# First layer-norm block of a transformer layer: V weights loaded as full-row slices, and two tiles transposed before they are centred

## The chip, the cores and the metric

The kernel runs on one core of one Trainium2 chip. The metric is the device time of one execution in microseconds. Before the change, three runs gave 692.64, 690.5 and 692.12 us, a median of 692.12 us. Data are bf16, accumulation is f32.

## The reference

A whole transformer layer is computed on 2048 rows of width 1024, with 32 heads of 32 columns, a causal window of 256 keys, and an MLP of width 3584:

```python
h  = x + attention(layernorm(x) @ wqkv) @ wo     # softmax over keys q-255 .. q
h2 = h + silu(layernorm(h) @ w1) @ w2
```

The layer norm has no weights: `(x - mean) / sqrt(var + 1e-5)`.

## The kernel before

The rows are worked in four blocks of 512, each of four tiles of 128 rows. TensorE (PE) needs the normalized rows transposed, `lnT_b`: eight pieces (kt) of 128 columns, each with the block's 512 rows beside one another. From these come V, tile by tile and half by half of 512 columns (`v_group`, L249: eight matmuls of 128x512), and Q and K, 128 output columns for all four tiles at a time (`qk_group`, L259). Attention of a block runs between the dense matmuls of the next one, then come the output projection (L280) and the MLP (L673, L710).

Every engine takes its instructions in the order in which the program writes them (`tc.manual_schedule()`), so the order of the lines is the order of each engine's queue: PE (matmuls and transposes), DVE (VectorE), ACT (ScalarE), POOL (GpSimd), and SP, which issues nearly all DMAs. Accumulators in PSUM are taken in turn by `next_acc` (L239): two banks normally, four while the first block's V is made (L476), and six from the MLP on (L668), when the four banks of the attention scores (`sc`) join. The counter that chooses the bank, `acc_n`, runs through the whole program.

The change lies in the first block, which has nothing to hide its start behind:

- **Loads (L155 to L163).** SP issues tile 0 of x, then V's first 512 columns in four pieces of 256 KB (two kt each), tile 2, the other 512 columns in two pieces of 512 KB with tile 3 between them, and the first quarter of the Q and K weights. ACT issues tile 1.
- **Warming (L172 to L176).** Two calls of `busy` run f32 matmuls on zeros, of 512 and 384 columns, before the data are there.
- **Tiles 0 and 1.** The mean is summed half on ACT and half on DVE (L464), DVE centres the tile in four quarters (L471), PE transposes it in pairs of kt (`turn_first`, L220), and ACT or DVE copies the transposes out of PSUM into `lnT_b`. These tiles aren't scaled yet: PE multiplies centred rows by V's weights (L497 for the first 512 columns, L513 for the others), and the eviction to `v` on ACT multiplies with 1/std (L532, L538). The variance is a squaring pass on ACT (`var_first`, L477), and later DVE normalizes both tiles in place (`norm_first`, L484) and a transposing DMA (`ln_transpose`, L211) overwrites their part of `lnT_b` for Q and K.
- **Tile 2** is normalized in full first: statistics on DVE (`ln_stats`, L182), root on ACT (L215), reciprocal and normalization on DVE (L218, L208), PE transposes (`turn_some`, L515), copies on ACT and DVE.
- **Tile 3** goes the same way but is transposed by DMA.
- **Order.** `ORDER` (L42) lists PE's steps: a pair `(j, h)` transposes two kt of tile j, a triple `(j, k0, k1)` multiplies kt k0 to k1 of tile j by V's first half. Then follow, in the order of the lines L506 to L546, the second half for tiles 0 and 1 in two parts (`half_pair`) around tile 2's transposes and first half, tile 2's second half, and tile 3. At the end SP loads the other Q and K weights (L541), ACT loads the table of Exp (L544), and `qk_group` begins (L582).

Of the kernel before, what the change touches and what calls it, by code (L numbers as in the profile page):

```python
# [8 lines left out]
BF16 = mybir.dt.bfloat16  # L9
F32 = mybir.dt.float32  # L10
I32 = mybir.dt.int32
ACT = mybir.ActivationFunctionType
ALU = mybir.AluOpType

P = 128
# [23 lines left out]
    [(1, "Y", 2), (2, "C", 1), (3, "Y", 3)],  # L39
]  # L40
SPLIT = [(0, 8), (8, 16), (16, 21), (21, 27), (27, 32)]
ORDER = [  # L42
    (0, 0), (0, 1), (0, 2), (0, 0, 2), (0, 3), (0, 2, 4), (1, 0), (0, 4, 6), (1, 1), (1, 2), (1, 3), (1, 0, 4),
    (1, 4, 6), (0, 6, 8), (1, 6, 8),
]


# [1 line left out]
def kernel(  # L49
# [88 lines left out]
    def load_x(b, j, queue=nc.sync):  # L138
        queue.dma_start(out=x_ring[(b % 2) * 4 + j], in_=x2d[(b * 4 + j) * P:(b * 4 + j + 1) * P, :])

    def load_wqkv(c0, parts=1, queues=(nc.sync,)):
        dst = wqk[:, :, c0:c0 + 512] if c0 < 2 * D else wv[:, :, c0 - 2 * D:c0 - 2 * D + 512]
        n = KT // parts
        for k in range(0, KT, n):
            queues[k // n % len(queues)].dma_start(out=dst[:, k:k + n, :], in_=wqkv_v[:, k:k + n, c0:c0 + 512])
# [8 lines left out]

    load_x(0, 0)  # L155
    load_x(0, 1, nc.scalar)
    load_wqkv(2 * D, 4)
    load_x(0, 2)
    for k in (0, 4):
        nc.sync.dma_start(out=wv[:, k:k + 4, 512:1024], in_=wqkv_v[:, k:k + 4, 2 * D + 512:3 * D])  # L160
# [11 lines left out]
    def busy(n):  # L172
        nc.tensor.matmul(o_ps[0][:].rearrange("p (a c) b -> p a (c b)", c=2)[:, 0:n], lhsT=warm, rhs=wide[:, 0:n], start=True, stop=True)

    for n in (4, 3):
        busy(n)  # L176


# [35 lines left out]
    def ln_root(st, rs, j):  # L214
        nc.scalar.activation(out=rs[:, j:j + 1], in_=st[:, j, 1:2], func=ACT.Sqrt, bias=eps[:], scale=1.0)  # L215

    def ln_recip(rs, j):
        nc.vector.reciprocal(out=rs[:, j:j + 1], in_=rs[:, j:j + 1])  # L218

    def turn_first(j, h, src, copy):  # L220

        for i in range(2):
            kt = h * 2 + i
            nc.tensor.transpose(out=tp_ps[h][:, i * P:(i + 1) * P], in_=src[:, kt * P:(kt + 1) * P], identity=ident[:])
        n = 2 if j or h else 1
        for i in range(0, 2, n):
            copy(out=lnT_b[0][:, h * 2 + i:h * 2 + i + n, j * P:(j + 1) * P],
                 in_=tp_ps[h][:, i * P:(i + n) * P].rearrange("p (k q) -> p k q", q=P))

    def ln_tiles(tag):  # L230
        st = small.tile([P, 4, 2], F32, name=f"st_{tag}", tag=f"st_{tag}")
# [7 lines left out]
    def next_acc():  # L239
        acc_n[0] += 1  # L240
        return acc_banks[acc_n[0] % len(acc_banks)]
# [213 lines left out]


    st, rs = ln_tiles("a")
    x_mid = [view(r_e, 1024 + 1024 * j, 1024) for j in range(2)]
    scrap = view(r_e, 3072, 1024)
    scrap_v = view(r_e, 4096, 512)  # L460
    mean = small.tile([P, 6], F32, name="mean")
    var = small.tile([P, 2], F32, name="var")

    def half_mean(j, h, engine):  # L464
        x, m = x_ring[j][:, h * 512:(h + 1) * 512], mean[:, j * 2 + h:j * 2 + h + 1]
        if engine is nc.scalar:
            engine.activation(out=scrap[:, 0:512], in_=x, func=ACT.Identity, scale=-1.0 / D, accum_out=m)
        else:
            engine.tensor_scalar(out=scrap_v, in0=x, scalar1=-1.0 / D, scalar2=None, op0=ALU.mult, op1=ALU.add, accum_out=m)

    def center(j):  # L471
        for h in range(4):
            out, in0 = (x[j][:, h * 256:(h + 1) * 256] for x in (x_mid, x_ring))
            nc.vector.tensor_scalar(out=out, in0=in0, scalar1=mean[:, j * 2:j * 2 + 1], scalar2=mean[:, j * 2 + 1:j * 2 + 2], op0=ALU.add, op1=ALU.add)

    acc_banks += [o[:].rearrange("p a b -> p (a b)") for o in o_ps]  # L476
    def var_first(j):  # L477

        nc.scalar.activation(out=scrap, in_=x_ring[j], func=ACT.Square, bias=mean[:, j + 4:j + 5], scale=1.0, accum_out=var[:, j:j + 1])

    def root_first(j):
        nc.scalar.activation(out=rs[:, j:j + 1], in_=var[:, j:j + 1], func=ACT.Sqrt, bias=eps[:], scale=1.0 / D)

    def norm_first(j):  # L484
        nc.vector.tensor_scalar(out=x_ring[j], in0=x_ring[j], scalar1=mean[:, j + 4:j + 5], scalar2=rs[:, j:j + 1], op0=ALU.add, op1=ALU.mult)

    for j in range(2):
        half_mean(j, 1, nc.scalar)
        half_mean(j, 0, nc.vector)
        center(j)  # L490
    nc.vector.tensor_tensor(out=mean[:, 4:6], in0=mean[:, 0:4:2], in1=mean[:, 1:4:2], op=ALU.add)
    first = [next_acc() for _ in range(2)]
    for step in ORDER:
        if len(step) == 3:
            j, k0, k1 = step
            for kt in range(k0, k1):
                nc.tensor.matmul(first[j], lhsT=lnT_b[0][:, kt, j * P:(j + 1) * P], rhs=wv[:, kt, 0:512], start=(kt == 0), stop=(kt == KT - 1))  # L497
        else:
            turn_first(*step, x_mid[step[0]], dve if step[0] and step[1] > 1 else act)
    var_first(0)  # L500
    ln_stats(x_ring[2], st, 2)
    ln_root(st, rs, 2)
    var_first(1)
    ln_recip(rs, 2)
    ln_norm(x_ring[2], st, rs, 2)
    pair = [next_acc() for _ in range(2)]  # L506

    def half_pair(k):
        for j in range(2):
            for kt in range(k, k + 4):  # L510
                if (k, j, kt) == (0, 1, 3):
                    turn_some(0, 2, 0, 2)
                nc.tensor.matmul(pair[j], lhsT=lnT_b[0][:, kt, j * P:(j + 1) * P], rhs=wv[:, kt, 512:1024], start=(kt == 0), stop=(kt == KT - 1))  # L513

    def turn_some(bank, j, k0, k1, copy=act):  # L515
        for kt in range(k0, k1):
            nc.tensor.transpose(out=tp_ps[bank][:, (kt - k0) * P:(kt - k0 + 1) * P], in_=x_ring[j][:, kt * P:(kt + 1) * P], identity=ident[:])
        copy(out=lnT_b[0][:, k0:k1, j * P:(j + 1) * P], in_=tp_ps[bank][:, 0:(k1 - k0) * P].rearrange("p (k q) -> p k q", q=P))

    ln_stats(x_ring[3], st, 3)  # L520
    half_pair(0)
    turn_some(1, 2, 2, 4)
    turn_some(2, 2, 4, 8, dve)
    ln_root(st, rs, 3)
    for j in range(2):
        root_first(j)
    ln_recip(rs, 3)
    ln_norm(x_ring[3], st, rs, 3)
    ln_recip(rs, 0)
    ln_recip(rs, 1)  # L530
    for j in range(2):
        nc.scalar.activation(out=v[:, j, 0:16, 0:DH], in_=first[j].rearrange("p (h d) -> p h d", d=DH), func=ACT.Identity, scale=rs[:, j:j + 1])  # L532
    v_group(0, 2, 0, act, acc=tp_ps[3][:].bitcast(F32))
    norm_first(0)
    norm_first(1)
    half_pair(4)
    for j in range(2):
        nc.scalar.activation(out=v[:, j, 16:32, 0:DH], in_=pair[j].rearrange("p (h d) -> p h d", d=DH), func=ACT.Identity, scale=rs[:, j:j + 1])  # L538
    for j in (3, 0, 1):
# [4 lines left out]
    nc.scalar.activation(out=dummy[:], in_=eps[:], func=ACT.Exp)  # L544
    v_group(0, 3, 0, act)
    v_group(0, 3, 1, act)  # L546
# [216 lines left out]
```

## Time and profile before

| | |
|---|---|
| runs | 692.64, 690.5, 692.12 us; median 692.12 us |
| profiled execution, first to last instruction (span) | 688.4 us |
| median less span | 3.7 us |
| PE busy | 674.8 us, 98% |
| DVE, ACT, POOL busy | 292.2, 244.0, 160.6 us |
| granted TensorE clock, mean | 1.000 |
| DMA | 61.48 MB, mean 89 GB/s |

The profile is that of one execution; for the profiled execution itself only the span is given. A busy PE isn't PE at its peak, since matmuls overlap in the pipeline. In a timeline row stand the start, the time to the end of the last instruction of the group, the engine, the line, the operation, the output and inputs, the count, and in brackets the idle time of the engine before and what ended it. A row of the chain gives start, length, what, and how many.

### The profile page before, as it was taken

Reading aid. Unit: us, or ns where it says so; the run is one execution under the profiler, and the core shown is the slowest. Engines: PE = TensorE matmul, PEld = TensorE weight load, DVE = VectorE, ACT = ScalarE, POOL = GpSimd, SP = SyncE. Lnnn points to the kernel's source line nnn. Section 1 sums busy time; section 2 is a strip of 40 time slices with the busy share of each in tenths; the row PEclk is TensorE's granted clock in tenths of the full one; section 3 lists DMA queues with packets and bytes.
Section 4 is the critical chain, followed back from the end, with each engine's and each line's share of the span. In section 5 each row is a group of like instructions: output and inputs, shape, how many; then the busy total and the mean of one; then the engine's idle time right before and its main releaser. Section 6 shows DMA issues by size and latency. Waiting matters only on the chain.

```text
span 688.4 us, 14116 instructions
## 1 busy us (share of the span) xinstructions
PE 674.8 (98%) x5890; PEld 341.9 (50%) x6004; DVE 292.2 (42%) x614; ACT 244.0 (35%) x465; POOL 160.6 (23%) x295
## 2 busy tenths in 40 slices
PE   9999999999999999999999999999999999999998
PEld 4445555555555555544444444444444444444445
DVE  5267647744444459434316133342233251333111
ACT  6326666667666666421300033300133100233000
POOL 1016665566666656400000000000000000000000
PEclk9999999999999999999999999999999999999999
DMA  8842242136241888781023310023300124100110
GB/s 272 262 64 69 42 89 51 29 60 186 71 131 28 254 246 236 177 313 61 17 88 113 83 39 0 1 91 72 82 0 1 34 83 91 39 1 1 30 39 24
DMA packets 78640, 61.48 MB, mean 89 GB/s; under 512 B 52464, under 2 KB 62704, under 8 KB 78576
## 3 DMA queue, kind: packets, MB, share of 16 engines
q1 hardware_dynamic: 78432, 60.31, 31.7%
q8 instruction: 47, 0.77, 0.5%
q10 hardware_dynamic: 144, 0.26, 0.1%
q14 instruction: 17, 0.14, 0.1%
HBM read 39.85 MB, written 8.39 MB: 70 GB/s over the span
## 4 chain that ended last, share of the span: by engine, by line
PE 98%; issue 1%; DMA 0%; DVE 0%; DVEq 0%
PE hacc L673 19%; PE acc L259 16%; PE hacc L710 14%; PE acc L710 14%; PE acc L673 9%; PE acc L280 7%; PE acc L249 6%; PE o_ps L392 5%; PE sc L312 3%; PE hacc L280 1%; PE sc L364 1%; PE sc L338 1%; PE o_ps L249 1%; DMA r_o<-in_A_x_dram 0%; PE acc L497 0%
## 5 line engine op out<-in xcount | busy, mean ns | idle before, releaser
L382 POOL TENSOR_SCALAR_AFFINE_SELECT r_e<-r_e 128x512 bf16<-128x512 bf16 (+1 forms) x288 | 157.6, 562 | 123.6 <-ACT r_e L372 60.3
L710 PEld LDWEIGHTS <-r_a 128*128 128x128 bf16 x952 | 90.9, 98 | 103.0
L673 PEld LDWEIGHTS <-r_w 128*128 128x128 bf16 x896 | 87.3, 98 | 104.8
L673 PE MATMUL hacc<-r_e,r_w 128*128 128x512 bf16 x468 | 104.9, 379 | 0.5
L710 PE MATMUL hacc<-r_a 128*128 128x512 bf16 (+1 forms) x496 | 100.2, 361 | 0.4
L710 PE MATMUL acc<-r_a 128*128 128x512 bf16 (+1 forms) x439 | 94.5, 372 | 0.5
L324 ACT ACTIVATE r_e<-sc 128x768 bf16<-128x768 f32 x96 | 78.2, 814 | 47.6 <-PE sc L312 46.6
L682 ACT ACTIVATE r_n<-hacc 128x512 f32<-128x512 f32 x30 | 17.9, 597 | 178.9 <-PE hacc L673 177.8
L259 PEld LDWEIGHTS <-r_w 128*128 128x128 bf16 x512 | 47.1, 98 | 55.0 <-issue 1.0
L261 DVE CAST r_a<-acc 128x512 bf16<-128x512 f32 x56 | 38.7, 692 | 57.4 <-PE acc L259 54.8
L259 PE MATMUL acc<-r_t,r_w 128*128 128x512 bf16 x233 | 56.5, 380 | 2.4 <-issue 1.7
L259 PE MATMUL acc<-r_w 128*128 128x512 bf16 x240 | 56.0, 379 | 1.5 <-issue 0.9
L392 PEld LDWEIGHTS <-r_e 128*128 128x128 bf16 x1440 | 47.4, 96 | 17.9
L392 PE MATMUL o_ps<-r_a,r_e 128*128 128x33 bf16 x1440 | 48.1, 178 | 0.0
L280 PE MATMUL acc<-r_o,r_a 128*128 128x512 bf16 x188 | 46.3, 380 | 1.9 <-issue 1.1
L673 PE MATMUL acc<-r_e,r_w 128*128 128x512 bf16 x191 | 43.3, 379 | 0.2
L725 DVE SCALAR_TENSOR_TENSOR r_t<-acc,r_t 128x512 bf16<-128x512 f32 (+1 forms) x16 | 10.6, 665 | 69.3 <-PE acc L710 63.9
L325 ACT ACTIVATE r_e<-sc 128x256 bf16<-128x256 f32 x96 | 37.6, 392 | 0.0
L280 PEld LDWEIGHTS <-r_a 128*128 128x128 bf16 x256 | 23.4, 98 | 27.0
L683 DVE SCALAR_TENSOR_TENSOR r_a<-r_n,hacc 128x512 bf16<-128x512 f32 x30 | 20.6, 687 | 33.1 <-ACT r_n L682 33.1
L683 DVE SCALAR_TENSOR_TENSOR r_a<-r_a,hacc 128x512 bf16<-128x512 f32 x30 | 20.6, 687 | 31.2 <-ACT r_a L682 31.2
L725 DVE SCALAR_TENSOR_TENSOR r_t<-hacc,r_t 128x512 bf16<-128x512 f32 (+1 forms) x18 | 11.6, 647 | 51.7 <-PE hacc L710 51.7
(104 smaller groups left out, 546.7 us busy)
## 6 DMA issues: line engine op xcount, KB each, us to landing
r_w<-in_B_w_dram SPq DMA_DIRECT2D x8, 896.0 KB, 5.9
r_a<-in_B_w_dram SPq DMA_DIRECT2D x7, 1024.0 KB, 8.0
r_w<-in_A_wqkv_dram SPq DMA_DIRECT2D x4, 1024.0 KB, 9.0
h_dram<-r_t SPq DMA_DIRECT2D x16, 256.0 KB, 2.4
r_t<-h_dram SPq DMA_DIRECT2D x16, 256.0 KB, 2.9
out_dram<-r_t SPq DMA_DIRECT2D x31, 128.0 KB, 1.7
r_o<-in_A_x_dram SPq DMA_DIRECT2D x15, 256.0 KB, 4.2
r_e<-h_dram SPq DMA_DIRECT2D x3, 1024.0 KB, 5.6
```

The source lines that it names most:

```text
L249: nc.tensor.matmul(acc, lhsT=lnT_b[b % 2][:, kt, j * P:(j + 1) * P], rhs=wv[:, kt, c * 512:(c + 1) * 512], start=(kt == 0), stop=(kt == KT ...
L259: nc.tensor.matmul(acc, lhsT=wqk[:, kt, col0:col0 + P], rhs=lnT_b[b % 2][:, kt, :], start=(kt == 0), stop=(kt == KT - 1))
L261: copy(out=(qT, kT)[which][b][:, g, :], in_=acc)
L280: nc.tensor.matmul(acc, lhsT=qT[b][:, g, j * P:(j + 1) * P], rhs=wo[:, g, c * 512:(c + 1) * 512], start=(g == 0), stop=(g == G - 1))
L324: nc.scalar.activation(out=tri[:, :, :, 64:256], in_=both, func=ACT.Exp, scale=scale)
L325: nc.scalar.activation(out=e[:, 1024:1280].rearrange("p (h q) -> p h q", q=P), in_=bank[:, :, 192:320], func=ACT.Exp, scale=scale)
L382: nc.gpsimd.affine_select(out=dst, in_=src, pattern=[[0, n] for n in dst.shape[1:-1]] + [[sgn, P]], compare_op=ALU.is_ge if upper else ALU ...
L392: nc.tensor.matmul(o_ps[pair][:, qt * 2 + hh, 0:VW], lhsT=chunk_of(i, bank, piece, pair, hh), rhs=v[:, b * 4 + kt, g * 4 + pair * 2 + hh, ...
L673: nc.tensor.matmul(acc, lhsT=w1[:, kt, ft * P:(ft + 1) * P], rhs=ln2T[b][:, kt, :], start=(kt == 0), stop=(kt == KT - 1))
L683: nc.vector.scalar_tensor_tensor(out=gT[:, ft, :], in0=th, scalar=1.0, in1=acc, op0=ALU.add, op1=ALU.mult)
L710: nc.tensor.matmul(acc[:, 0:c1 - c0], lhsT=gT[:, ft, j * P:(j + 1) * P], rhs=w2[ft // 4][:, ft % 4, c0:c1], start=(ft == 0), stop=(ft == F ...
L725: nc.vector.scalar_tensor_tensor(out=t_out[j % 2][:, c0:c1], in0=acc[:, 0:c1 - c0], scalar=0.5, in1=t_in[j % 2][:, c0:c1], op0=ALU.mult, o ...
```

## The change

- V's weights come in eight slices of 256 KB, one kt with all 1024 columns each (rows of 2 KB in place of 1 KB). Tile 2 is issued behind slice 3 and tile 3 behind slice 4.
- The second warming call is cut from 384 columns to 128.
- Of tiles 0 and 1, PE transposes kt 2 to 7 as loaded, before the mean is known. Kt 0 and 1 are centred first (`center_first`) and transposed then (`turn_mid`). For the others, the negative mean is brought from a column to a row by two small matmuls against the identity (`spread_mean`; the mean split into two bf16 parts), copied to SBUF (`m_row`), and added by DVE while it copies the transposes out of PSUM (`center`), two kt at a time.
- Tile 0's mean is still made by halves on ACT and DVE; tile 1's is one pass on ACT.
- Tile 2's mean, variance and root are on ACT, behind tile 0's variance; tile 1's variance comes after them. Tile 3's statistics stay on DVE.
- PE's order (`FIRST`): each slice of weights is used for both column halves of tiles 0 and 1 when its turn comes, in four accumulators; `(1,)` and `(2,)` stand for tile 1's centred transposes and its mean row with everything that follows on DVE and ACT; the steps with "turn" transpose half of tile 2 each. Then tile 2's and tile 3's V as whole groups.
- Tile 3's transposing DMA is issued ahead of those of tiles 0 and 1 as before, all of them written behind tile 2's steps. `next_acc` is called six times in the block in place of seven.

```diff
-ORDER = [
...
+FIRST = [
+    (0, 0), (0, 1), (1,), (0, 2), (2,), (0, 3), (1, 0), (1, 1), (1, 2), (1, 3),
+    (0, 4), (1, 4), (0, 5), (1, 5), (0, 6), (1, 6), (2, 0, 4, "turn"), (0, 7), (2, 4, 8, "turn"), (1, 7),
 ]
...
     load_x(0, 0)
     load_x(0, 1, nc.scalar)
-    load_wqkv(2 * D, 4)
-    load_x(0, 2)
-    for k in (0, 4):
-        nc.sync.dma_start(out=wv[:, k:k + 4, 512:1024], in_=wqkv_v[:, k:k + 4, 2 * D + 512:3 * D])
-        if k == 0:
-            load_x(0, 3)
+    for k in range(KT):
+        nc.sync.dma_start(out=wv[:, k, :], in_=wqkv_v[:, k, 2 * D:3 * D])
+        if k in (3, 4):
+            load_x(0, k - 1)
     load_wqkv(0)
...
-    for n in (4, 3):
+    for n in (4, 1):
         busy(n)
...
+    x_mid = [view(r_e, 1024 + 256 * j, 256) for j in range(2)]
+    m_row = [view(r_e, 4608 + 256 * j, 256).bitcast(F32) for j in range(2)]
+    spread = [t[:].bitcast(F32) for t in tp_ps[2:]]
+
+    def neg_mean(out, x):
+        nc.scalar.activation(out=scrap[:, 0:x.shape[-1]], in_=x, func=ACT.Identity, scale=-1.0 / D, accum_out=out)
+
+    def low_part(j):
+        m = mean[:, j:j + 1]
+        nc.vector.tensor_tensor(out=low[:, j:j + 1], in0=m, in1=m.bitcast(BF16)[:, 1:2], op=ALU.subtract)
+
+    def spread_mean(j):
+        parts = (mean[:, j:j + 1].bitcast(BF16)[:, 1:2], low[:, j:j + 1])
+        for n, m in enumerate(parts):
+            nc.tensor.matmul(spread[j][:, 0:P], lhsT=m.to_broadcast([P, P]), rhs=ident[:], start=(n == 0), stop=(n == 1))
+
+    def turn(bank, off, j, k0, k1):
+        for kt in range(k0, k1):
+            nc.tensor.transpose(out=tp_ps[bank][:, off + (kt - k0) * P:off + (kt - k0 + 1) * P],
+                                in_=x_ring[j][:, kt * P:(kt + 1) * P], identity=ident[:])
+
+    def center_first(j, a, b=None):
+        nc.vector.tensor_scalar(out=x_mid[j], in0=x_ring[j][:, 0:256], scalar1=a, scalar2=b, op0=ALU.add, op1=ALU.add if b is not None else ALU.bypass)
...
+    def center(j, k0):
+        m = m_row[j]
+        nc.vector.tensor_tensor(out=lnT_b[0][:, k0:k0 + 2, j * P:(j + 1) * P],
+                                in0=tp_ps[j][:, k0 * P:(k0 + 2) * P].rearrange("p (k q) -> p k q", q=P),
+                                in1=bass.AP(tensor=m.tensor, offset=m.offset, ap=[m.ap[0], [0, 2], m.ap[1]]), op=ALU.add)
...
+    turn(0, 2 * P, 0, 2, 8)
+    turn(1, 2 * P, 1, 2, 8)
+    neg_mean(mean[:, 6:7], x_ring[0][:, 512:1024])
+    nc.vector.tensor_scalar(out=scrap_v, in0=x_ring[0][:, 0:512], scalar1=-1.0 / D, scalar2=None, op0=ALU.mult, op1=ALU.add,
+                            accum_out=mean[:, 7:8])
+    neg_mean(mean[:, 1:2], x_ring[1])
+    center_first(0, mean[:, 6:7], mean[:, 7:8])
+    nc.vector.tensor_tensor(out=mean[:, 0:1], in0=mean[:, 6:7], in1=mean[:, 7:8], op=ALU.add)
+    low_part(0)
+    turn_mid(0)
+    copy_mid(0, dve)
+    spread_mean(0)
+    dve(out=m_row[0], in_=spread[0][:, 0:P])
+    center(0, 2)
+    center_first(1, mean[:, 1:2])
+    low_part(1)
+    center(0, 4)
+    first = [[next_acc() for _ in range(2)] for _ in range(2)]
+
+    def slices(j, k, *cs):
+        for c in cs or (0, 1):
+            nc.tensor.matmul(first[j][c], lhsT=lnT_b[0][:, k, j * P:(j + 1) * P], rhs=wv[:, k, c * 512:(c + 1) * 512],
+                             start=(k == 0), stop=(k == KT - 1))
+
+    for n, step in enumerate(FIRST):
+        if step == (1,):
+            turn_mid(1)
+            copy_mid(1, act)
+            center(0, 6)
+        elif step == (2,):
+            spread_mean(1)
+            act(out=m_row[1], in_=spread[1][:, 0:P])
+            for k in (2, 4, 6):
+                center(1, k)
+            var_first(0)
+            neg_mean(mean[:, 2:3], x_ring[2])
+            var_first(2)
+            root_first(2)
+            ln_stats(x_ring[3], st, 3)
+            ln_root(st, rs, 3)
+            ln_recip(rs, 2)
+            norm_first(2)
+            ln_recip(rs, 3)
+            ln_norm(x_ring[3], st, rs, 3)
+            var_first(1)
+        elif len(step) == 4:
+            j, k0, k1, _ = step
+            turn(k0 // 4, 0, j, k0, k1)
+            dve(out=lnT_b[0][:, k0:k1, j * P:(j + 1) * P], in_=tp_ps[k0 // 4][:, 0:512].rearrange("p (k q) -> p k q", q=P))
         else:
+            slices(*step)
     for j in range(2):
         root_first(j)
+        ln_recip(rs, j)
+    ln_transpose(x_ring[3], lnT_b[0], 3)
     for j in range(2):
+        norm_first(j)
     for j in range(2):
+        for c in range(2):
+            nc.scalar.activation(out=v[:, j, c * 16:(c + 1) * 16, 0:DH], in_=first[j][c].rearrange("p (h d) -> p h d", d=DH),
+                                 func=ACT.Identity, scale=rs[:, j:j + 1])
+    for j in range(2):
         ln_transpose(x_ring[j], lnT_b[0], j)
     for c0 in (D, 512, D + 512):
         load_wqkv(c0)
-    v_group(0, 2, 1, act)
+    v_group(0, 2, 0, act, acc=spread[0])
+    v_group(0, 2, 1, act, acc=spread[1])
     nc.scalar.activation(out=dummy[:], in_=eps[:], func=ACT.Exp)
```

More of the change, by code (lines that the diff above doesn't have):

```diff
@@ L218, in ln_recip @@
         nc.vector.reciprocal(out=rs[:, j:j + 1], in_=rs[:, j:j + 1])
[L220 to L228, printed above, removed]
     def ln_tiles(tag):
@@ L457 @@
     st, rs = ln_tiles("a")
-    x_mid = [view(r_e, 1024 + 1024 * j, 1024) for j in range(2)]
     scrap = view(r_e, 3072, 1024)
     scrap_v = view(r_e, 4096, 512)
[L461 to L474, printed above, removed]
-    acc_banks += [o[:].rearrange("p a b -> p (a b)") for o in o_ps]
+    mean = small.tile([P, 8], F32, name="mean")
+    low = small.tile([P, 2], BF16, name="low")
+    var = small.tile([P, 3], F32, name="var")
+    acc_banks += [o[:].rearrange("p a b -> p (a b)") for o in o_ps]
@@ L500 @@
[L500 to L524, printed above, removed]
+        nc.vector.tensor_scalar(out=x_ring[j], in0=x_ring[j], scalar1=mean[:, j:j + 1], scalar2=rs[:, j:j + 1], op0=ALU.add, op1=ALU.mult)
```

33 lines of the change are left out of this document (6 added, 27 removed).

## The prediction

> **What bounds the kernel now.** I read the page first: the share of each engine and the chain that ended last.
>
> ```profile
> span 688.4 us, 14116 instructions
> PE 674.8 (98%) x5890; PEld 341.9 (50%) x6004; DVE 292.2 (42%) x614; ACT 244.0 (35%) x465; POOL 160.6 (23%) x295
> PE 98%; issue 1%; DMA 0%; DVE 0%; DVEq 0%
> ```
>
> PE carries 98% of the chain. An edit therefore counts only if it alters how much PE does, or when PE has to stand still. The change touches the first 21 us, so the second view is the chain of that stretch (start, length, what, count).
>
> ```profile
> 0.81 2.79 DMA r_o<-in_A_x_dram
> ...
> 4.43 0.36 DVE r_e L474
> ...
> 4.83 0.80 PE tp L224 x6
> 5.63 0.56 PE acc L497 x2
> ...
> 12.04 0.14 issue
> ...
> 17.31 3.45 PE o_ps L249 x16
> 20.76 0.43 PE acc L259 x2
> ```
>
> The reader sees a load, a mean, a centring, and then PE without a break but 0.14 us from 4.83 to 20.76, where the Q and K products (L259) begin. The wait at 12.04 is the only gap left to close. So the change is worth what it does to one moment: when the first L259 matmul can start. Whatever stands after that moves with it. A 512-column matmul costs 3.45/16 = 0.216 us.
>
> The third view is the timeline of the engines, with durations of single instructions.
>
> ```profile
> 4.83 0.55 PE L224 MATMUL tp<-ident,r_e 128*128 128x128 bf16 x4 [0.35 <-DVE r_e L474]
> 7.21 0.50 PE L224 MATMUL tp<-ident,r_e 128*128 128x128 bf16 x6
> L224 PE MATMUL tp<-ident,r_e x16: 219/219/311, 4.8 to 7.5; 128*128 128x128 bf16 x16
> 5.58 0.61 PE L497 MATMUL acc<-r_w 128*128 128x512 bf16 x2
> 20.60 15.70 PE L259 MATMUL acc<-r_w 128*128 128x512 bf16 x70
> ```
>
> One transpose lasts 0.219 us, but they follow one another closely: (0.50 - 0.22)/5 = 0.056 us apart at 7.21, and (0.55 - 0.22)/3 = 0.11 us apart at 4.83. PE runs at half pace until about 5.2 us. The stretch that I sum runs from the first V matmul (5.58) to the first L259 (20.60): 15.02 us. In it lie 64 V matmuls, 64 x 0.216 = 13.82, and the 20 transposes left of 24, 20 x 0.056 = 1.12; the sum is 14.94, so 0.08 us are slack.
>
> **The change part by part.**
>
> *PE work.* After the first V matmul the changed kernel still has the 64 matmuls, but of transposes only tile 1's two centred ones and tile 2's eight (10 x 0.056 = 0.56), and the second mean's two spreading matmuls of 128 columns (0.11; not in this trace, priced as transposes, the nearest row; at 512 columns they would cost 0.43). Sum 13.82 + 0.56 + 0.11 + 0.08 = 14.57 against 15.02: **-0.45 us**. The twelve raw transposes and the first spread come before.
>
> *The start.* Tile 0's mean is made as before, and the first centring still ends near 4.8. But PE's queue holds tile 1's six raw transposes ahead of the two centred ones, and these wait for tile 1's load.
>
> ```profile
> 3.62 0.69 DVE L469 TENSOR_SCALAR_CACHE_REDUCE r_e<-r_o 128x512 bf16<-128x512 bf16 x1 [2.54 <-DMA r_o<-in_A_x_dram]
> 4.00:5.00 1.00, 0.65 (x3) 0.13 (x2) 0.89 (x5) 0.96 (x4) 0.00 (x0) 1.00 1.03 315
> 5.00:6.00 1.00, 1.00 (x8) 0.49 (x7) 1.00 (x4) 0.84 (x6) 0.00 (x0) 1.00 1.06 366
> 10.00:11.00 1.00, 1.00 (x6) 0.41 (x5) 0.90 (x3) 1.00 (x3) 0.00 (x0) 1.00 1.10 350
> ```
>
> Tile 0 is there at 3.60. The windows (last column GB/s) show 315 to 366, so a piece of 256 KB takes 0.72 to 0.83 us: tile 1 comes at about 4.35, its transposes at half pace take 6 x 0.11 = 0.66, and the centred pair starts near 5.0 instead of 4.83: **+0.17 us**, first matmul at 5.75.
>
> *Weights.* The order is now x0, x1, slices 0 to 3, x2, slice 4, x3, slices 5 to 7. By 0.72 to 0.78 a piece the slices come at about 5.1, 5.8, 6.6, 7.3, 8.8, 10.3, 11.0, 11.8. PE asks for slice 0 at 5.75, 1 at 6.18, 2 at 6.72 (after two transposes), 3 at 7.27, 4 at 9.4, 5 at 10.3, 6 at 11.1, 7 after tile 2's first transposes. Slices 2, 3 and 5 are close. From 0 to 0.4 us; I take **+0.1**. SP's three extra issues cost 1.95/4 = 0.49 us each on a queue that is otherwise waiting:
>
> ```profile
> 1.27 1.95 SPq L145 DMA_DIRECT2D r_w<-in_A_wqkv_dram  x4
> SPq L160 <- DMA r_w<-in_A_wqkv_dram: 0.3, 1, 0.3
> 13.39 4.18 SPq L212 DMA_TRANSPOSE r_w<-r_o  x3
> ```
>
> The second row is an issue that had to wait for an earlier landing, and the changed kernel has more such issues. Still, six pieces are under way by then, so the engines aren't short of work.
>
> *Centring at the copy.* Tile 0's copy moves to DVE and each later pair of slices is one DVE addition of a 128x256 piece in PSUM and the mean row.
>
> ```profile
> 7.70 0.49 DVE L227 COPY r_w<-tp 128x256 bf16<-128x256 bf16 x2 [0.27 <-PE tp L224]
> 281.11 0.42 DVE L404 TENSOR_TENSOR r_n<-o_ps,recip 128x256 bf16<-128x256 f32 x1
> ```
>
> Such an addition isn't in this trace; a copy of that size takes 0.25, a multiplication out of PSUM 0.42, and I take the middle, 0.34, since it has the copy's bf16 source and the multiplication's second operand. DVE does copy, mean row, addition, tile 1's centring, its low part, addition, addition: from 5.4 to about 7.2, ahead of PE by 0.3 us or more at every use. Tile 1's additions start at 7.8 and end at 8.9, used from 8.5, two slices at a time. I cost them at nothing; the cover is PE's own work on slices 0 to 3.
>
> *Tile 2's statistics.* Before, they were on DVE and beside ACT's variances. Now all are in ACT's queue: mean row of tile 1, variance of tile 0, mean of tile 2, variance of tile 2, root. Each is a pass over 1024 columns.
>
> ```profile
> 7.79 1.15 ACT L479 ACTIVATE r_e<-r_o,mean 128x1024 bf16<-128x1024 bf16 x1
> 8.84 0.19 ACT L479 ACTIVATION_READ_ACCUMULATOR r_e<-r_o,mean 128x1 f32 x1
> 9.74 0.29 ACT L215 ACTIVATE rs_a<-st_a,eps 128x1 f32<-128x1 f32 x1 [0.71 <-DVE st_a L188]
> 10.07 0.16 DVE L218 RECIPROCAL rs_a<-rs_a 128x1 f32<-128x1 f32 x1 [0.36 <-ACT rs_a L215]
> 10.27 0.55 DVE L208 TENSOR_SCALAR r_o<-r_o,st_a,rs_a 128x1024 bf16<-128x1024 bf16 x1
> 11.00 0.31 PEld L517 LDWEIGHTS <-r_o 128*128 128x128 bf16 x2
> 6.98 0.37 ACT L227 COPY r_w<-tp 128x256 bf16<-128x256 bf16 x1 [0.27 <-PE tp L224]
> 10.73 1.28 DVE L180 BATCH_NORM_STATS2 ln_st<-r_o 128x6 f32<-128x512 bf16 x2
> 12.04 0.21 DVE L188 BATCH_NORM_AGGREGATE st_a<-ln_st 128x2 f32<-128x12 f32 x1
> ```
>
> A pass with its read is 8.84 + 0.19 - 7.79 = 1.24 us. From root to PE's weight load is 11.00 - 9.74 = 1.26. PE ends the second spread at 5.75 + 0.86 + 0.11 + 0.1 + 0.43 + 0.11 = 7.36. ACT sees it 0.2 later and copies 128x128 in about 0.26 (less than the 0.37 of 128x256): 7.82. Three passes: 11.54. Tile 2 is on PE's doorstep at 12.80. PE reaches its transposes after 28 matmuls: 5.75 + 6.05 + 0.11 + 0.11 + 0.1 = 12.12. **It waits 0.7 us**, with four matmuls of slice 7 queued behind that don't need tile 2. Bounds: 0 if the passes overlap more or PE is late anyway, 1.2 if DVE, which takes tile 3's statistics (1.28 + 0.21 after x3's landing) ahead of the reciprocal, is late too.
>
> *Behind it.*
>
> ```profile
> r_w<-r_o SPq DMA_TRANSPOSE x3, 3.3
> 14.06 0.68 ACT L532 ACTIVATE r_a<-o_ps,rs_a 128x512 bf16<-128x512 f32 x1
> 17.95 1.28 ACT L544 ACT_TABLE_LOAD   x1
> ```
>
> Tile 3's transposing DMA is issued at about 13.3 (before 13.39). Tiles 0 and 1 follow from 15.2, when DVE has normalized them, 4.18/3 = 1.4 apart, so that the last lands near 16.6 + 3.3 = 19.9, ahead of L259. The second weight block behind them on SP is needed four groups, 6.9 us, after L259 starts. ACT's four evictions start at 14.7 behind DVE's last reciprocals and at 0.68 end by 17.4; two copies and the table load (1.28) then end near 20, and the copy of tile 3's first half by 20.7. Its bank is the first that L259 writes, so L259 can't start before that, which holds for the quick rival only. I cost all this at nothing: the cover is the 32 matmuls (6.9 us) of tiles 2 and 3, and without it, each late microsecond would cost one.
>
> *A shift far away.* The changed block asks for six accumulators in turn instead of seven. The turn goes on through the program, so at the first MLP group (L673) PE gets the last bank of the score space instead of a free one.
>
> ```profile
> 283.02 0.41 ACT L325 ACTIVATE r_e<-sc 128x256 bf16<-128x256 f32 x1
> 283.08 1.89 PE L673 MATMUL acc<-r_a,r_w 128*128 128x512 bf16 x8
> ```
>
> That bank is read by ACT until 283.43, and PE wants it at 283.08: **+0.4 us**, from 0 (were another bank first) to 0.4.
>
> Sum: -0.45 + 0.17 + 0.1 + 0.7 + 0.4 = **+0.9 us**. It is made against the profiled execution, span 688.4; the runs' median of 692.12 lies 3.7 us above and I carry that unchanged: 693.0. The runs themselves lie 2.1 us apart, so such a sum is no more than a lean.
>
> **The rivals.**
>
> *Tile 2 in time.* PE doesn't stand at 12.1, since ACT gets there earlier or since the slices make PE late by as much. Without the 0.7 the sum is +0.2, without the bank -0.2: 691.9 to 692.3. For it: three ACT passes are all that separates them. Against: nothing in ACT's queue lets tile 2 pass tile 0's variance.
>
> *The clock stays low* (slower). The warming matmuls (1792 columns in four records) end at 4.47 now; cut to 1280 columns they end about 3.35 x 512/1792 = 0.96 us earlier, and what replaces them are short transposes with waits for x0 and x1 between.
>
> ```profile
> 1.12 3.35 PE L173 MATMUL o_ps<-r_e 128*128 128x512 f32 x4 [1.12 <-DVE eps L151]
> ```
>
> Full pace came near 5.2, some 4.0 us after 1.12. If the sparser stretch isn't counted and PE needs as long again, 4.0 us of work run at half pace and 2.0 us are lost: 693.0 + 2.0 = 695.0, slower by 0.4%. It decides once PE's gaps between 3.5 and 5.0 add up to clearly more than the 0.35 us of now. Against it: at half pace the twelve transposes themselves fill 1.3 us of these 1.5. The Trainium skill, "TensorE: Matmul & The Clock Gate", Part 1 on the clock gate, says that the clock is released after a busy window of about 3.4 us which runs freely; the rows above agree with a release near 4 us. By the page's window a missed release would cost an estimated 1.7 us, 694.7.
>
> *Weights late.* Every slice now serves four matmuls, so PE eats them at 0.86 us a piece where before it had other tiles' work to put between. If the waiting issues make slices 5 to 7 a microsecond later, PE loses about 0.5 us more in part hidden by tile 2: 693.5.
>
> **How the numbers follow.** Forecast (693.0) 0.56; tile 2 in time 0.22; clock 0.10; weights late 0.12. About 0.3%, 2.1 us, is what a measurement of this kernel can tell from no change. The forecast, the first rival and the late weights lie within it; of slower by more there is nearly all of the clock's 0.10 and the upper tail of the forecast and of the late weights, 0.05; of faster 0.03, since the whole -0.45 of PE work is far too small for it. Range: from 691.2 (first rival's -0.2 and most of the runs' scatter) to 694.8 (the unknown costs at their upper ends, 0.3 + 0.5 above the forecast, and scatter); it leaves out half of the clock's case and small tails.
>
> **What would show it.** First V matmul near 5.75, and the transposes before it 0.11 us apart. An idle stretch of PE of 0.5 to 0.9 us before tile 2's transposes, its releaser DVE's normalization; first L259 at 21.0 to 21.3. At L673 a short wait for ACT L325. V matmuls 0.216 us apart from the first on; if they stand 0.43 apart, the clock rival holds. If L259 starts before 20.4 or after 22, the working is wrong; likewise if the difference arises after 21 us other than at L673.

## The result, and the profile after

The changed kernel takes 691.79 us (median of 22 runs, 690.91 to 693.64). The kernel before, measured beside it, takes 690.62 us (22 runs, 690.11 to 692.64); the median of the three runs known ahead was 692.12. The ratio is 1.0015, 95% interval 1.0008 to 1.0022: slower by 0.15%, 1.0 us, with 0.6 and 1.5 us as the ends (the two medians lie 1.2 us apart). The prediction had +0.9 us, within 0.3%. Its 693.0 in absolute terms lies 1.2 us above the measured time, since it was counted from 692.12.

The page of the changed kernel, its first lines:

```profile
span 690.4 us, 14121 instructions
PE 676.1 (98%) x5893; PEld 342.9 (50%) x6008; DVE 291.1 (42%) x612; ACT 244.6 (35%) x462; POOL 160.8 (23%) x295
```

PE is the bound as before. The span of this execution is 2.0 us longer than that of the one before. The chain of waits in the first block shows the first part of it (start, length, what, count):

```profile
1.13 3.30 DMA r_o<-in_A_x_dram
4.43 0.05 issue
4.48 0.82 PE tp L471 x6
...
5.90 0.61 PE acc L520
6.51 0.43 PE o_ps L520
6.93 0.43 PE acc L520
7.36 0.33 PE o_ps L520
7.69 0.11 PE tp L479 x2
7.80 0.22 PE acc L520
...
8.38 0.02 ACT r_e L530
8.40 0.14 issue
8.54 0.06 ACT r_e L491
...
9.82 1.16 ACT r_e L458 x2
10.97 0.02 issue
11.00 1.25 ACT r_e L491 x2
12.25 0.02 issue
12.27 0.30 ACT rs_a L494
12.57 0.02 issue
12.60 0.17 DVE rs_a L216
12.77 0.03 issue
12.80 0.56 DVE r_o L497
13.35 0.05 issue
13.40 0.40 PE tp L471 x4
```

Three things stand here that the chain of before doesn't have. The chain goes over tile 1's load to its raw transposes, and the first V matmul comes at 5.90 instead of 5.58. The matmuls are 0.43 us apart until 7.4 and 0.22 from then on: PE ran at half pace for longer in this execution. And from 8.38 on the chain leaves PE for ACT's passes over tiles 0 and 2 and DVE's normalization of tile 2. The timeline of PE at that place:

```profile
12.71 0.38 PE L520 MATMUL acc<-r_w 128*128 128x512 bf16 x1
13.40 0.40 PE L471 MATMUL tp<-ident,r_o 128*128 128x128 bf16 x4 [0.30 <-DVE r_o L497]
...
21.62 2.75 PE L247 MATMUL acc<-r_w 128*128 128x512 bf16 x11
```

The next instruction could have followed at 12.71 + 0.22 = 12.93 and came at 13.40: 0.47 us of waiting for tile 2. The bracket says 0.30, since it counts from the modelled end of the matmul. The first Q product (now L247) comes at 21.62 instead of 20.60. The rest of the difference arises far behind the change. In the timeline at the first MLP group:

```profile
284.33 0.40 ACT L313 ACTIVATE r_e<-sc 128x256 bf16<-128x256 f32 x1
...
284.79 1.89 PE L695 MATMUL hacc<-r_a,r_w 128*128 128x512 bf16 x8 [0.24 <-ACT r_e L313]
```

PE waits for the last exponential on the bank that it got. And in the output projection the chain leaves PE once more, which it doesn't before:

```profile
271.47 0.61 DVE r_t L270
272.08 0.04 issue
272.12 0.59 PE acc L268 x2
```

To follow all runs I read the same marks off each timeline: the starts of the first V matmul, of the first Q matmul, of the last output projection matmul ahead of the MLP and of the first MLP matmul, and the time at which the matmuls' distance falls from 0.43 to 0.22 us (the step of the granted clock in the trace). I call that time full pace, what lies ahead of it half pace, and the stretch from the first Q matmul to the last projection matmul the projection stretch. The names of the runs stand with the experiments below; all times are in us.

| run | full pace from | first V | first V to first Q | first Q to last projection | last projection to first MLP | ratio to before (interval) |
|---|---|---|---|---|---|---|
| before | 5.15 | 5.58 | 15.02 | 262.26 | 0.22 | |
| changed | 7.46 | 5.90 | 15.72 | 262.55 | 0.62 | 1.0015 (1.0008, 1.0022) |
| e1_bank | 5.07 | 5.69 | 14.98 | 262.74 | 0.22 | 1.0007 (0.9999, 1.0016) |
| e2_tile2_first | 4.45 | 5.63 | 15.60 | 262.74 | 0.62 | 1.0015 (1.0006, 1.0023) |
| e3_warm_again | 4.65 | 5.79 | 15.12 | 262.54 | 0.62 | 1.0018 (1.0009, 1.0026) |
| e4_before_again | 6.88 | 5.56 | 15.54 | 262.26 | 0.22 | 1.0008 (0.9997, 1.0019) |
| e5_before_lanes | 7.21 | 5.70 | 15.64 | 262.26 | 0.22 | 1.0000 (0.9991, 1.0009) |
| e6_order | 4.15 | 5.33 | 15.26 | 262.75 | 0.61 | 1.0016 (1.0008, 1.0025) |
| e7_all | 7.44 | 5.88 | 15.34 | 262.75 | 0.22 | 1.0000 (0.9991, 1.0008) |
| e8_before_short_warm | 7.54 | 5.45 | 15.92 | 262.26 | 0.22 | 1.0017 (1.0008, 1.0025) |
| e9_before_pad | before 5.6 | 5.63 | 15.31 | 262.75 | 0.22 | 1.0008 (0.9998, 1.0017) |
| e10_short_warm_2 | 7.46 | 5.42 | 15.90 | 262.27 | 0.21 | one run, 690.87 us |
| e11_leaner | 8.90 | 5.66 | 16.03 | 262.27 | 0.22 | 1.0011 (1.0002, 1.0020) |
| e12_leaner_dense | 8.02 | 5.78 | 15.52 | 262.27 | 0.22 | 1.0009 (1.0000, 1.0018) |

Behind the first MLP matmul all are alike (402.70 us to PE's last). From before to changed the marks give 0.32 + 0.70 + 0.29 + 0.40 = 1.71 us of the span's 2.0. Most of the rest, 0.23, lies behind PE's last matmul (2.65 us before, 2.88 changed); e5, the kernel before with two small DMAs more, has 2.87 there, so that part isn't the change's. The time of full pace differs between executions of one kernel, so single profiles differ by up to a microsecond for that reason alone: a V stretch is comparable only after about half the time from the first V matmul to full pace is taken off. That gives 14.88 to 15.02 for the kernel before and its repetitions (e4 and e5), 14.94 for the changed kernel. e9's 15.31 at full pace has another reason: a piece of V's weights landed at 7.08 instead of 6.74 and set PE's pace.

### The profile page after: what moved, and what is told of

Read it like the earlier page. It is cut to its first block, busy times and chain, and to the rows that moved or that the text cites. A ratio compares the mean times of both kernels' runs of the same rounds, so it can differ in the third digit from the quotient of the medians.

```text
span 690.4 us, 14121 instructions
## 1 busy us (share of the span) xinstructions
PE 676.1 (98%) x5893; PEld 342.9 (50%) x6008; DVE 291.1 (42%) x612; ACT 244.6 (35%) x462; POOL 160.8 (23%) x295
## 4 chain that ended last, share of the span: by engine, by line
PE 93%; DVE 2%; issue 2%; DMA 2%; ACT 1%; SPq 0%; DVEq 0%
PE hacc L695 19%; PE hacc L732 18%; PE acc L247 16%; PE acc L732 10%; PE acc L695 9%; PE acc L237 6%; PE o_ps L380 5%; PE acc L268 4%; PE sc L300 2%; PE hacc L268 1%; DMA h_dram<-r_t 1%; PE sc L352 1%; DVE r_t L270 1%; DVE ln_st L178 1%; PE tp L237 1%
## 5 line engine op out<-in xcount | busy, mean ns | idle before, releaser
L732 PE MATMUL hacc<-r_a 128*128 128x512 bf16 (+1 forms) x578 | 123.4, 371 | 0.5
L695 PE MATMUL hacc<-r_e,r_w 128*128 128x512 bf16 x442 | 100.0, 379 | 0.7
L247 PEld LDWEIGHTS <-r_w 128*128 128x128 bf16 x512 | 47.2, 98 | 55.0 <-issue 1.0
L732 PE MATMUL acc<-r_a 128*128 128x512 bf16 (+2 forms) x358 | 72.2, 358 | 0.4
L704 ACT ACTIVATE r_n<-acc 128x512 f32<-128x512 f32 x15 | 9.0, 597 | 162.0 <-PE acc L695 162.0
L247 PE MATMUL acc<-r_t,r_w 128*128 128x512 bf16 x233 | 56.5, 380 | 2.4 <-issue 1.7
L247 PE MATMUL acc<-r_w 128*128 128x512 bf16 x240 | 56.0, 379 | 1.5 <-issue 0.9
L747 DVE SCALAR_TENSOR_TENSOR r_t<-hacc,r_t 128x512 bf16<-128x512 f32 (+1 forms) x21 | 14.1, 672 | 90.4 <-PE hacc L732 85.1
L268 PE MATMUL acc<-r_o,r_a 128*128 128x512 bf16 x196 | 48.3, 380 | 2.0 <-issue 1.1
L695 PE MATMUL acc<-r_e,r_w 128*128 128x512 bf16 x216 | 49.1, 379 | 0.0
L695 PE MATMUL hacc<-r_a,r_w 128*128 128x512 bf16 x149 | 34.4, 379 | 0.4 <-ACT r_e L313 0.2
L705 DVE SCALAR_TENSOR_TENSOR r_a<-r_n,hacc 128x512 bf16<-128x512 f32 x27 | 18.6, 687 | 28.1 <-ACT r_n L704 28.1
```

Of the source, the lines that this page charges most:

```text
L247: nc.tensor.matmul(acc, lhsT=wqk[:, kt, col0:col0 + P], rhs=lnT_b[b % 2][:, kt, :], start=(kt == 0), stop=(kt == KT - 1))
L268: nc.tensor.matmul(acc, lhsT=qT[b][:, g, j * P:(j + 1) * P], rhs=wo[:, g, c * 512:(c + 1) * 512], start=(g == 0), stop=(g == G - 1))
L695: nc.tensor.matmul(acc, lhsT=w1[:, kt, ft * P:(ft + 1) * P], rhs=ln2T[b][:, kt, :], start=(kt == 0), stop=(kt == KT - 1))
L705: nc.vector.scalar_tensor_tensor(out=gT[:, ft, :], in0=th, scalar=1.0, in1=acc, op0=ALU.add, op1=ALU.mult)
L732: nc.tensor.matmul(acc[:, 0:c1 - c0], lhsT=gT[:, ft, j * P:(j + 1) * P], rhs=w2[ft // 4][:, ft % 4, c0:c1], start=(ft == 0), stop=(ft == F ...
L747: nc.vector.scalar_tensor_tensor(out=t_out[j % 2][:, c0:c1], in0=acc[:, 0:c1 - c0], scalar=0.5, in1=t_in[j % 2][:, c0:c1], op0=ALU.mult, o ...
```

## The experiments

The theory at the start of them: three places carry the difference, tile 2's wait, the bank at the first MLP group, and PE's half pace by the shorter warming. The main rival: the first block alone makes it, by half pace or late slices. The ratio's interval is some 0.0008 each way, about 0.6 us, and the kernel before measured against itself (e4 below) came out at 1.0008, so the traces decide where a theory names less.

**One more accumulator in turn (e1_bank).** On the changed kernel:

```diff
     v_group(0, 3, 1, act)
+    next_acc()
     del acc_banks[2:]
```

> The changed kernel with one more accumulator taken in turn at the end of the first block, so that the first MLP group gets the bank that it had before. Theory (the shift of the accumulators costs 0.4 us at the first MLP group): no wait for ACT there, the distance to the kernel before between the last projection group and the first MLP group goes from +0.40 to 0, and the time falls by 0.4 us, ratio to before 1.0009 where the change has 1.0015. Rival (the first block alone makes the difference, and PE's wait at the MLP is given back later): the time stays at 1.0015.

The wait at the MLP is gone (0.22), and the ratio fell to 1.0007; its interval (0.9999 to 1.0016) can't tell that from 1.0015, so the trace carries this. PE's timeline there now names a free bank, and PE no longer waits for the exponential that ends at 283.97:

```profile
283.56 0.41 ACT L313 ACTIVATE r_e<-sc 128x256 bf16<-128x256 f32 x1
283.62 0.81 PE L696 MATMUL acc<-r_a,r_w 128*128 128x512 bf16 x3
```

The 0.40 us of the shift are shown. The same run, with full pace at 5.07, has 14.98 from first V to first Q, against 15.02: with half pace out of the way the first block is worth nothing from its first V matmul on, and still has its wait for tile 2 (0.43). But its stretch to the last projection is 0.48 longer, although the bank's turn is as before. That was new.

**Tile 2's passes first (e2_tile2_first).** On the changed kernel:

```diff
-            var_first(0)
             neg_mean(mean[:, 2:3], x_ring[2])
             var_first(2)
             root_first(2)
+            var_first(0)
```

> The changed kernel with ACT's order altered: tile 2's mean, variance and root come ahead of tile 0's variance. Theory (tile 2 comes late because a pass of 1.24 us over tile 0 stands before it): tile 2's normalization starts 0.8 us or more earlier, bounded by tile 3's statistics on DVE, PE's wait before tile 2's transposes goes from 0.5 to 0, and the first Q product comes 0.5 us earlier; ratio 1.0008. Rival (the half pace of PE at the start carries the loss, and the wait only hides in it): PE's wait goes, but something else ends last in its place, tile 0's variance and the evictions, and the first Q product moves by less than 0.2 us.

The chain of this run:

```profile
1.72 5.20 DMA r_w<-in_A_wqkv_dram
6.93 0.04 issue
6.97 0.38 PE acc L520
...
12.96 0.22 PE acc L520
13.18 0.22 PE tp L471 x4
```

Tile 2's transposes follow the matmul before them without a gap, and DVE is no longer in the chain: the wait is gone, as the theory had it. But slice 1 landed at 6.93 in this execution (5.66, 6.57 and 6.24 in e1, the changed kernel and e3), the second pair of matmuls waited 0.9 us for it, and the ratio stayed at 1.0015. The theory was right about the wait. What removing it is worth alone stays open: in this profile the third rival of the prediction, late weights, took its place, the interval (1.0006 to 1.0023) takes in the 1.0008 that was expected, and how often a slice is that late isn't known from one profile per kernel.

**The long warming again (e3_warm_again).** `for n in (4, 3)` in the changed kernel.

> The changed kernel with the second warming call at 384 columns again. Theory (the cut warming lets the clock come late): full pace near 5.2 us instead of 7.5, the first four V matmuls 0.22 us apart instead of 0.43, against which the raw transposes start 0.9 us later and push the first V matmul by 0.3 to 0.6 us; in all 0 to 0.5 us faster, ratio 1.0008 to 1.0015. Rival (the time of full pace varies from execution to execution by itself): full pace comes at a time that has nothing to do with the warming, and the time is worse by the later transposes, 1.0018.

Full pace at 4.65, but others with the short warming have 4.15, 4.45, 5.07 and 7.44 and the changed kernel 7.46. The ratio isn't better, 1.0018. In the changed kernel the cut costs nothing that can be seen; the rival held here.

**The kernel before again (e4_before_again).**

> The kernel before once more, unaltered, for a second profile of its start and for the scatter. Theory (the warming sets when full pace comes): full pace near 5.2 us again, ratio 1.000 with an interval under 0.001. Rival (it varies by itself): full pace at another time, up to 8.6 us, and V matmuls 0.43 us apart until then.

Full pace at 6.88 instead of 5.15, the first Q matmul at 21.10 instead of 20.60, everything behind it equal. So half a microsecond of a single profile's first block is chance. The rival held. The ratio, 1.0008 (0.9997 to 1.0019) for the same kernel, shows how little a ratio under 1.001 says.

**Two more DMAs (e5_before_lanes).** The kernel before with this behind block 1's x loads:

```diff
+    for i in range(2):
+        nc.sync.dma_start(out=r_n[0:1, 64 * i:64 * (i + 1)], in_=x2d[0:1, 64 * i:64 * (i + 1)])
```

> The kernel before with two more DMAs of 128 bytes (into a buffer not yet in use) behind block 1's x loads, so that as many DMAs stand ahead of the output projection as in the changed kernel; nothing else altered. Theory (between the first Q product and the last output projection group every profile with the change is 0.28 to 0.48 us longer, since DMAs take their completion semaphores in turn, eight of them, and two more DMAs in the first block shift all later ones, so that a residual load waits longer for its semaphore): this stretch goes from 262.26 to about 262.6, the rest stays, 0.05% slower. Rival (it follows from when the first block ends or from where its data lie): the stretch stays at 262.26.

The projection stretch is 262.26 and the ratio 1.0000. The theory of the semaphores' turn fell.

**Raw transposes behind the centred pair (e6_order).** The changed kernel with `turn(1, 2 * P, 1, 2, 8)` written behind `spread_mean(0)`.

> The changed kernel with tile 1's six raw transposes behind tile 0's centred pair and its mean row on PE, instead of ahead of them. Theory (the first V matmul waits for x1 by 0.1 to 0.3 us because PE takes its queue in order): first V matmul at 5.55 to 5.6 instead of 5.69 to 5.90; but the first Q product moves by 0.1 us at most, since tile 2's statistics, which start after tile 1's mean row, end last. Rival (the first matmul sets the end): the first Q product comes 0.1 to 0.3 us earlier at the same time of full pace.

The first V matmul comes at 5.33, and the first Q matmul at 20.59, 0.07 earlier than in e1, whose full pace was likewise ahead of its first V matmul. As the theory said, the early start is lost at tile 2, where PE waits 0.36 us, and here also at slice 2, which landed at 6.55. Ratio 1.0016, no gain. The early first V matmul belongs to this execution as well as to the order: e7, with the same order but at half pace, has it at 5.88.

**Everything undone (e7_all).** The edits of e1, e2 and e6 in one, and six small DMAs as in e5.

> The changed kernel with every suspected cost taken away: tile 1's raw transposes behind tile 0's centred pair, tile 2's passes ahead of tile 0's variance, one more accumulator in turn, and six more DMAs of 128 bytes, which bring the semaphores' turn to where it was. Theory: no wait for tile 2, 0.22 between the last projection group and the first MLP matmul, 262.26 between the first Q product and the last projection group, and the first Q product 0.3 to 0.5 us before that of the kernel before at the same time of full pace: ratio 0.9993 to 1.000. Rival (slices that come late decide, as in the run where one came at 6.93): the first block stays 0.3 us or more longer, ratio 1.0005.

Ratio 1.0000. There is no wait for tile 2 and none at the MLP:

```profile
12.87 0.22 PE acc L520
13.09 0.22 PE tp L471 x4
```

From first V to first Q it is 15.34 with full pace at 7.44; less half of 7.44 - 5.88 that is 14.56. The prediction's sum for the block without waits was 14.57. Yet the projection stretch is 262.75, so DMA counts are out as its cause a second time.

**The short warming in the kernel before (e8_before_short_warm, e10_short_warm_2).** `for n in (4, 1)`, nothing else, timed, and once more for a profile.

> The kernel before with the second warming call cut from 384 to 128 columns, nothing else. Theory (full pace comes at a time of its own in each execution, whatever the warming does): same time as before within 0.0006, full pace somewhere between 4.1 and 7.5 us. Rival (the shorter warming puts full pace off): full pace after 5.2 us in most executions, and slower by 0.2 to 1 us, ratio 1.0005 to 1.0015.

> The kernel before with the short warming once more, for a second sample of when full pace comes. Theory (without matmuls between 3.6 and 4.7 us no window ends busy before 7.5): full pace at 7.5 or later, up to 10.9 us. Rival (it comes at any time, whatever the warming): somewhere between 4.1 and 7.5.

Ratio 1.0017 (1.0008 to 1.0025): the cut alone makes the kernel before 1.1 us slower by the medians. PE's timeline of the first of the two:

```profile
1.12 2.50 PE L173 MATMUL o_ps<-r_e 128*128 128x512 f32 x4 [1.12 <-DVE eps L151]
4.70 0.91 PE L224 MATMUL tp<-ident,r_e 128*128 128x128 bf16 x6 [1.07 <-DVE r_e L474]
5.45 1.04 PE L497 MATMUL acc<-r_w 128*128 128x512 bf16 x2
```

PE idles 1.07 us ahead of the transposes, and the two matmuls at 5.45 are at half pace. Full pace came at 7.54 and 7.46, later than in any of the three profiles with the long warming (5.15, 6.88, 7.21), if by only 0.25 us over the latest of them. Both profiled executions were among their kernel's quickest (690.92 and 690.87 us, where the others reach 692.60), which fits that full pace comes later still in most; that last part is argued, no profile shows it. In the changed kernel the raw transposes of both tiles fill this gap: they start at 3.59, as the warming ends.

**Eight more PE instructions (e9_before_pad).** The kernel before with this behind the warming:

```diff
+    for i in range(4):
+        nc.tensor.transpose(out=tp_ps[3][:, i * P:(i + 1) * P], in_=ident[:], identity=ident[:])
```

> The kernel before with four transposes of the identity added behind the warming, into a bank not yet in use: eight more PE instructions at the start, as many as the four spreading matmuls of the change add, and nothing else. Theory (what all profiles with the change have in common between the first Q product and the last projection group is a PE program that is eight instructions longer, so that its 16 KB fetches of instructions fall elsewhere among the loads of the projection stage): this stretch goes from 262.26 to 262.5 to 262.8. Rival (it comes from something else in the first block): it stays at 262.26.

The pages count the instructions, in e4 (the kernel before) and then in this run:

```profile
PE 684.8 (99%) x6004; PEld 342.3 (50%) x6004; DVE 292.5 (42%) x614; ACT 244.0 (35%) x465; POOL 160.5 (23%) x295
```

```profile
PE 685.2 (99%) x6008; PEld 342.4 (50%) x6008; DVE 292.2 (42%) x614; ACT 244.0 (35%) x465; POOL 161.1 (23%) x295
```

e1, the changed kernel with another bank, has x6008 and x6008 as well. (The profiles of before and changed lack some matmul records, so their counts can't be compared.) Instructions come by a DMA queue of their own, of which the page of this run has packets, MB and share:

```profile
q8 instruction: 47, 0.77, 0.4%
```

The projection stretch is 262.75. Four transposes without use at 4 us lengthen the output projection, 250 us later, by 0.49 us; in the runs with the change it was 0.28 to 0.49. The place is the same too. DVE's timeline in the kernel before, then in this run:

```profile
256.70 0.69 DVE L282 TENSOR_TENSOR r_t<-acc,r_a 128x512 bf16<-128x512 f32 x1 [0.83 <-DMA h_dram<-r_t]
```

```profile
257.71 0.69 DVE L284 TENSOR_TENSOR r_t<-acc,r_a 128x512 bf16<-128x512 f32 x1 [1.50 <-DMA h_dram<-r_t]
```

The residual addition waits for a transfer, the store of an earlier row tile that still holds its buffer, 1.50 us instead of 0.83; DVE has no gap from there on, its evictions are late too, and at 271.6 PE waits for them. In the seven profiles with eight more instructions this wait is 1.33 to 1.68 us, in the seven without 0.29 to 0.83. On SP's own timeline the issue of MLP weights ahead of these transfers takes longer, in the kernel before and in this run:

```profile
246.78 0.50 SPq L590 DMA_DIRECT2D r_w<-in_B_w_dram  x1
```

```profile
247.13 1.46 SPq L592 DMA_DIRECT2D r_w<-in_B_w_dram  x1
```

But the longer issue isn't what makes the wait: in e6 it takes 0.50 us as before, and DVE waits 1.54. The store itself is under way longer. Counted from the first Q matmul it was issued at 229.24 in e6 and at 229.26 in e12, and landed at 236.72 and 235.61.

**The leaner block, twice (e11_leaner, e12_leaner_dense).** e7 without the small DMAs, with one bf16 mean instead of two parts (`low` now holds the mean rounded to bf16, and its low part is left out) and only the first warming call; then the same with the raw transposes ahead of the centred pair again. By the trace's count both have as many PE instructions as the kernel before: four more for the two spreading matmuls and their weight loads, four fewer for the warming call that is gone.

```diff
-    for n in (4, 1):
+    for n in (4,):
...
-        parts = (mean[:, j:j + 1].bitcast(BF16)[:, 1:2], low[:, j:j + 1])
+        parts = (low[:, j:j + 1],)
```

> The run with every suspected cost taken away, without the dummy DMAs, and leaner: the mean goes to the row as one bf16 number (its low part is left out, two small matmuls fewer) and the second warming call is gone. Theory (the first block now has nothing to wait for but its slices): first V matmul at 5.3 to 5.6, first Q product 0.1 to 0.2 us earlier than in the run before at the same time of full pace, about 20.2 to 21.1; if the fetches fall as in the kernel before, 262.26 in the middle stretch; ratio 0.9990 to 1.0000. Rival (the missing warming puts full pace off, or slices come late): full pace after 7.5 or V matmuls waiting, ratio 1.0005 or more.

> The leaner run with tile 1's six raw transposes back ahead of tile 0's centred pair, so that PE is busy between 4.3 and 5.0 us too. Theory (the leaner run lost by its late full pace, 8.9 us, since PE stood idle between its short matmuls): full pace between 4.1 and 7.5, first V matmul at 5.6 to 5.9, first Q product 20.3 to 21.1, 262.26 in the middle stretch and 0.22 before the MLP as in the kernel before; ratio 0.9992 to 1.0002. Rival (the one warming call is too little in any order): full pace after 7.5, ratio 1.0008 or more.

Both have 262.27 in the projection stretch: with the instruction count restored the loss is gone, and DVE's wait there is 0.39 in the first of the two:

```profile
257.35 0.69 DVE L270 TENSOR_TENSOR r_t<-acc,r_a 128x512 bf16<-128x512 f32 x1 [0.39 <-DMA h_dram<-r_t]
```

But full pace comes at 8.90 and 8.02, and the ratios are 1.0011 and 1.0009. Corrected for it, first V to first Q is 14.41 and 14.40, the shortest of all; what the block gains is lost again at half pace. In the denser order it came 0.9 us earlier, yet after 7.5: the rival of that run held, one warming call is too little in either order. No version here beats the kernel before.

## Why the prediction was right, point by point

The forecast was +0.9 us and a ratio within 0.3%; measured are +1.0 us (0.6 to 1.5). Its signs came out in part: the wait before tile 2's transposes, released by DVE's normalization, and the short wait for ACT at the first MLP group are there, but the difference also arises after 21 us at another place than L673, by which the prediction itself called its working wrong. By its terms:

- **PE work, -0.45.** Right: e7 has 14.56 at full pace where 14.57 was summed. Against the kernel before (14.88 to 15.02, corrected) that is -0.32 to -0.46.
- **The start, +0.17.** +0.32, +0.11, +0.05 and +0.21 in the four profiles with this order and two warming calls (changed, e1, e2, e3), 0.17 in the mean. The cause is in the changed kernel's chain, tile 1's load and its raw transposes. The size is less sure than that: the kernel before scatters from 5.56 to 5.70 in its own repetitions, and of the two runs with e6's order and two warming calls one has 5.33, the other (e7) 5.88.
- **Weights, +0.1.** The mean can't be told from these profiles. The landing of slice 1 scattered by 1.3 us, and in two of them (e2 and e6) a slice set the pace.
- **Tile 2, +0.7.** Right mechanism, size too big: 0.35 to 0.47 in four profiles (changed, e1, e3, e6), and none where tile 2's passes come first (e2, e7). PE's transposes follow the root by 1.13 us in the chain above (12.27 to 13.40), not 1.26 to the weight load, and ACT's mean row took 0.16 until the next pass (8.38 to 8.54), not 0.26.
- **The bank at the MLP, +0.4.** Exact: 0.40, and e1 takes it away.
- **Left out, +0.3 to +0.5.** The step that failed is the sentence that whatever stands behind the first Q product only moves with it, but for L673. The output projection grew by 0.28 to 0.49 us in all seven profiles of a program with eight more PE instructions ahead of it, by the change or by transposes without use, and in none of the seven without them. That an added instruction at the start acts there is shown (e9, e11, e12). Through what is argued. The page has instructions on a DMA queue of their own, 47 fetches of 16 KB. The traces show that the added instructions move these fetches: counted from the first Q matmul, one starts at 241.6 to 242.8 us in the seven profiles with eight more and at 244.0 to 244.4 in the seven without. The one ahead of DVE's long wait moves by less, 226.1 to 226.4 against 226.4 to 227.2. That a fetch is what delays the store isn't shown; no run moved a fetch alone.
- **The clock rival, 0.10.** Its condition, PE idling between the warming and the first real work, doesn't hold in the changed kernel, where the raw transposes fill the gap: e3 brings nothing. In the kernel before, where it holds, the same cut costs 0.17%. The sign that the prediction named for this rival, V matmuls 0.43 us apart, did show in the changed kernel's profile, until 7.46; but it shows in e4 and e5 too, with the warming of before, until 6.88 and 7.21, so it can't tell the two apart. The Trainium skill, "TensorE: Matmul & The Clock Gate", Part 1 on the clock gate, has the clock released by a freely running window of about 3.4 us. The nine profiles with the warming of before, or with raw transposes behind two warming calls, in which the step is recorded agree: they lie between 4.15 and 7.46, 3.3 us apart.

So the miss in tile 2 and the part left out nearly cancel. Up to the first Q product the sum had +0.5 us; the two profiles of the changed order at full pace from the start and without a late slice (e1, e3) have +0.06 and +0.31. Behind it the sum had +0.4, and the bank and the projection stretch make 0.7 to 0.9. The forecast's total is right by more than its parts deserve: that the two errors are of one size is luck.

## What to carry to other kernels

When PE is busy throughout, sum what is left on PE between two fixed marks, and compare profiles mark by mark after taking out the part at half pace; that resolved 0.15 us in the first block and 0.01 in the projection stretch, as long as no load came late, where the times resolved 0.6. An edit at the start also moves what is counted through the whole program, such as the turn of PSUM banks and the number of instructions, so look for the stages far behind where a wait is nearly due. If warming is cut, check that PE has other work right behind it.

## What the runs showed of the hardware that had not been expected

Four transposes without use, eight instructions, cost 0.49 us of waiting 250 us later. The Trainium skill, "Runtime: NRT & Kernel Launch", Instruction fetch mechanics, says that instructions are refilled in 16 KiB blocks over a DMA queue of the engine and that this is mostly hidden. The 47 fetches of 16 KB agree with it. PE wasn't seen to stop for one (in e1 it is busy for 684.5 of the 689.2 us, with 1.1 ahead of its first instruction and 2.9 behind its last); if the fetches are the link, which stays open, it is the stage's own transfers that paid.

In kernels with the same loads in the same order, one transfer landed up to 1.3 us apart from one execution to the next (slice 1: issued at 1.7 us each time, landed at 5.66 in e1 and 6.93 in e2).
